# A clustered-attention and two-MLP kernel: the first pair's argmax by heads, wide similarity passes, joined output adds, a new order table

## The chip, the cores and the metric

The kernel runs on one core of a Trainium2 chip. The metric is the device time of one execution in microseconds. Three timed runs of the kernel before have a median of 694.74 us (693.54 to 695.31). The profiled execution took 693.93 us; its span, from the first to the last recorded instruction, is 692.1 us.

## The reference, cut to what matters

```python
# 2 batches, 8 heads, 768 tokens, head size 64, 16 cluster centroids per head
q_assign = argmax(einsum('bhsd,hcd->bhsc', normalised q, normalised c))     # nearest centroid of each query
k_assign = argmax(einsum('bhsd,hcd->bhsc', normalised k, normalised c))
mask     = q_assign[..., :, None] == k_assign[..., None, :]
attn     = softmax(where(mask, q @ k.T / 8, -1e9))
x        = attn @ v                                   # (1536 tokens, 512)
h        = max(x @ w1, x @ w2, x @ w3)                # 512 -> 768
x        = h @ w_out                                  # 768 -> 512
out      = relu(x @ w_in) ** 2 @ w_out2               # 512 -> 2048 -> 512
```

## The kernel before, in words

Products are made in float32r. An operand is split into a rounded part and the rest ("high" and "low"), and a product takes three passes (high·high, high·low, low·high) that are summed in PSUM.

**Attention part** (about the first 254 us). The 16 heads are 8 pairs (numbered 0 to 7, `p`); each head has 6 query tiles of 128 rows, so there are 96 tiles (`s`), handled in groups of three (`g`, 32 of them). For a pair: load q and k, split them (`p_rq`, `p_rk`, `p_lq`, `p_lk`), copy the pieces by DMA into the stacked operands of the score products (`p_stack`), multiply with the centroids (`p_sim`, two token halves), scale into SBUF (`p_simc`, ScalarE), transpose (`p_argt`), find the argmax in five VectorE steps (`p_arg0` to `p_arg4`) which leave a one-hot tile, transpose that (`p_mkt`), and put it as extra mask rows into the score operands (`p_mq`, `p_mk` directly for the first head; `p_m4` and the DMAs of `p_md` for the others). For a tile: scores on TensorE (`a_scores`, L729 and L731), row maximum on VectorE (`a_max`, L738), exponential with row sums on ScalarE (`a_exp`, L745), normalisation mostly on GpSimd (`a_norm`, L763). For a group: six times three transposes (`a_tr`, L768), the high part (`a_hi`, ScalarE, L774), the low part (`a_lo`, VectorE, L779), two products with v (`a_av`, L788 and L789).

In PSUM there are two double banks (psd) for score tiles, three banks (pss) for transposes, similarities, argmax and masks, and one bank for the product with v.

The order of all these steps, on all engines, is one written list, `ATT_ORDER`; each engine runs its own steps in that order. `warm(n)` puts n matmuls that compute nothing between steps at the start, `WARM` says how many.

**MLP part** (to the end). The order comes from a planner, `arrange`, which uses costs and due times, shifted by a second list (`MOE_LATER`). TensorE is the engine that is planned for. The last stage, `outs`, adds for each of 8 pieces of the inner dimension (`g`, NG = 8) and each of 12 token tiles (`tk`) a product (`out_mm`, L1321) to an accumulator in SBUF (`acc`), on VectorE (L1349) or by seeding the bank with the accumulator on ScalarE and copying it back (L1346). After the last piece each token tile is stored (L1352).

Of the kernel before, what the change touches and what calls it, by code (L numbers as in the profile page):

```python
# [1439 lines left out]
```

## Time and profile before

| | |
|---|---|
| median of three runs | 694.74 us |
| profiled execution | 693.93 us, span 692.1 us |
| TensorE (PE) busy | 676.9 us, 98% |
| VectorE (DVE) busy | 561.2 us, 81% |
| ScalarE (ACT) busy | 501.1 us, 72% |
| GpSimd (POOL) busy | 210.0 us, 30% |
| last product with v ends (attention ends on TensorE) | 253.9 us |
| last matmul ends | 687.2 us |

Shares are averages over stages: the attention stage loads four engines, the MLP stage TensorE above all. A busy TensorE is not one at its peak: a matmul's record lasts longer than the distance to the next one, so short stalls don't show as idle time. The distance between starts tells more.

### The profile page before, as it was taken

To read this page: it belongs to the slowest core of one execution; us is meant where nothing else is said; L and a number is where in the kernel's file an instruction comes from. 1 tells how busy PE (TensorE), PEld (TensorE's weight loads), DVE (VectorE), ACT (ScalarE), POOL (GpSimd) and SP (SyncE) were. 2 spreads that over 40 slices of the span, in tenths; PEclk is the share of its full clock that TensorE was granted. 3 is DMA by queue.
4 is the path that set the end of the run, shared out by engine and by line. 5 is a ranking of instruction groups with operands and counts; after the bars stand their busy time and mean duration, and the time that the engine had idled before them with its cause. 6 is when DMAs were issued, how large, how long until landed. Compare 5 with 4: busy or idle time off the path is not lost.

```text
span 692.1 us, 10148 instructions
## 1 busy us (share of the span) xinstructions
PE 676.9 (98%) x3531; PEld 577.3 (83%) x3531; DVE 561.2 (81%) x906; ACT 501.1 (72%) x977; POOL 210.0 (30%) x242
## 2 busy tenths in 40 slices
PE   7899999999999999999999999999999999999997
PEld 6689889899999878888888888888888888888885
DVE  6898999999999979998979659889679585968433
ACT  6899989899999865575545547798877786776610
POOL 6477987988769770100000000000000010000010
PEclk9999999999999999999999999999999999999999
DMA  7884553726432002211311231112211203120012
GB/s 207 198 234 119 120 161 91 189 58 147 111 89 91 1 1 93 91 62 61 103 66 61 76 121 62 61 62 82 101 62 61 98 27 115 48 79 1 1 73 111
DMA packets 22004, 62.21 MB, mean 90 GB/s; under 512 B 3616, under 2 KB 5280, under 8 KB 21504
## 3 DMA queue, kind: packets, MB, share of 16 engines
q1 hardware_dynamic: 21232, 59.98, 29.3%
q10 hardware_dynamic: 720, 1.57, 0.7%
q8 instruction: 28, 0.46, 0.3%
q14 instruction: 24, 0.20, 0.1%
HBM read 38.83 MB, written 3.15 MB: 61 GB/s over the span
## 4 chain that ended last, share of the span: by engine, by line
PE 62%; DVE 2%; issue 1%; ACT 1%; POOL 0%; ACTq 0%; POOLq 0%
PE pss L1066 23%; PE psn L1066 18%; PE pss L1321 10%; PE psn L1321 8%; PE pss L1142 1%; DVE acc_acc L1349 1%; DVE at L779 0%; DVE wtv L399 0%; PE pss L768 0%; ACT e L745 0%; PE pss L788 0%; PE pss L789 0%; POOL xT L822 0%; PE psn L1142 0%; PE psn L425 0%
## 5 line engine op out<-in xcount | busy, mean ns | idle before, releaser
L779 DVE TENSOR_TENSOR at<-pss,at 128x384 fp32r<-128x384 f32 x192 | 100.0, 548 | 13.1 <-ACT at L774 12.4
L763 POOL TENSOR_SCALAR e<-e,nm 128x768 f32<-128x768 f32 x93 | 85.6, 934 | 47.2 <-DVE nm L753 32.6
L738 DVE TENSOR_REDUCE nm<-psd 128x1 f32<-128x768 f32 x96 | 90.6, 948 | 5.4 <-PE psd L731 3.7
L774 ACT CAST at<-pss 128x384 fp32r<-128x384 f32 x192 | 86.5, 483 | 9.3 <-PE pss L768 7.4
L745 ACT ACTIVATE e<-psd,nm 128x768 f32<-128x768 f32 x96 | 87.3, 910 | 4.1 <-DVE nm L738 3.5
L768 PE MATMUL pss<-ident,e 128*128 128x128 f32 x576 | 86.5, 275 | 3.4 <-DVE at L779 1.7
L768 PEld LDWEIGHTS pss<-ident,e 128*128 128x128 f32 x576 | 68.6, 140 | 15.2 <-DVE at L779 5.0
L788 PE MATMUL pss<-at,vs 128*128 128x384 f32 x192 | 71.2, 371 | 0.5 <-ACT avt L801 0.5
L1321 PE MATMUL pss<-w_wh,g_g 128*128 128x512 f32 x216 | 71.4, 389 | 0.0
L789 PE MATMUL pss<-at,vs 128*128 128x384 f32 x192 | 65.8, 343 | 0.4 <-DVE at L779 0.3
L1057 POOL TENSOR_TENSOR t_tt<-a_a,t_tt 128x256 f32<-128x256 f32 x3 | 2.5, 848 | 191.5 <-DVE t_tt L1054 191.5
L1321 PE MATMUL psn<-w_wh,g_g 128*128 128x512 f32 (+1 forms) x172 | 56.5, 384 | 0.0
L1321 PEld LDWEIGHTS pss<-w_wh,g_g 128*128 128x128 f32 x216 | 40.5, 188 | 8.4
L1066 PE MATMUL pss<-xT,w_wh 128*128 128x512 f32 x140 | 43.1, 389 | 0.0
L1321 PE MATMUL pss<-w_wl,g_g 128*128 128x512 f32 x108 | 42.0, 389 | 0.0
L1042 ACT CAST w_wh<-a_a 128x1024 fp32r<-128x1024 f32 (+1 forms) x28 | 28.6, 1020 | 14.9 <-DVE a_a L1036 14.9
L789 PEld LDWEIGHTS pss<-at,vs 128*128 128x128 f32 x192 | 36.4, 189 | 3.0 <-DVE at L779 2.5
L1025 ACT ACTIVATE a_a<-raw_raw 128x512 f32<-128x512 f32 (+1 forms) x56 | 36.4, 653 | 3.3 <-DMA raw_raw<-w 1.3
L1321 PEld LDWEIGHTS psn<-w_wh,g_g 128*128 128x128 f32 x172 | 32.1, 188 | 6.4
L788 PEld LDWEIGHTS pss<-at,vs 128*128 128x128 f32 x192 | 36.2, 189 | 1.4 <-issue 0.5
L1027 ACT ACTIVATE r_r<-raw_raw 128x512 uint32<-128x512 uint32 (+1 forms) x56 | 36.5, 651 | 0.7 <-PE pss L1066 0.7
L1030 DVE SCALAR_TENSOR_TENSOR a_a<-raw_raw,a_a 128x512 uint32<-128x512 uint32 (+1 forms) x56 | 35.6, 668 | 0.5
(249 smaller groups left out, 1743.0 us busy)
## 6 DMA issues: line engine op xcount, KB each, us to landing
raw_raw<-w SPq DMA_DIRECT2D x16, 512.0 KB, 4.0
raw_raw<-win SPq DMA_DIRECT2D x16, 512.0 KB, 4.0
raw_raw<-wo SPq DMA_DIRECT2D x16, 512.0 KB, 3.6
raw_raw<-wo SPq DMA_DIRECT2D x8, 384.0 KB, 3.3
out<-acc_acc SPq DMA_DIRECT2D x11, 256.0 KB, 2.0
tv<-vv SPq DMA_DIRECT2D x7, 384.0 KB, 3.3
stodd<-rl SPq DMA_DIRECT2D x12, 192.0 KB, 5.5
stodd<-rl SPq DMA_DIRECT2D x4, 576.0 KB, 7.9
```

Of the source, the lines that this page charges most:

```text
L738: dve.tensor_reduce(nms[g][:, 0, i : i + 1], pss[s][:, :, :HS], axis=AX.XY, op=ALU.max, negate=True)
L745: act.activation(two(e), pss.pop(s)[:, :, :HS], AF.Exp, bias=nm[:, 0, i : i + 1], accum_out=nm[:, 1, i : i + 1])
L763: (pool if w == "P" else dve).tensor_scalar(e, e, r, 1.0, op0=ALU.mult, op1=ALU.mult)
L768: pe.transpose(pt[:, i * P : (i + 1) * P], et[3 * g + i][:, kt * P : (kt + 1) * P], ident)
L774: act.copy(a[:, 0, :], pts[g, kt][:, :HS])
L779: eng.tensor_tensor(a[:, 1, :], pts.pop((g, kt))[:, :HS], f(a[:, 0, :]), op=ALU.subtract)
L788: pe.matmul(avs[g][:, :HS], l, a[:, 0, :], start=kt == 0, stop=False)
L789: pe.matmul(avs[g][:, :HS], l, a[:, 1, :], start=False, stop=kt == NQ - 1)
L1025: op(("ab", u), due - 9, {A_: act_t(n) + 0.03}, lambda e, raw=raw, c=c: e.activation(T[a][:, c], f(T[raw][:, :n, 1]), AF.Abs), [("ld", u)] ...
L1027: op(("rd", u), due - 7.5, {A_: act_t(n) + 0.03}, lambda e, raw=raw, c=c: e.mul(u32(T[r][:, c]), T[raw][:, :n, 0], float(2.0**-29)), [("ld ...
L1066: pe.matmul(T[bank], T[w[wi]][:, wb * P : wb * P + P], x(xi), start=first and n == 0, stop=last and n == 3 * len(ks) - 1, skip_group_check ...
L1321: pe.matmul(T[bank][:, : n.stop - n.start], T["g", 2 * g + j, c][:, a_, i * P : i * P + P], T[wt, u][:, 512 * j + n.start : 512 * j + n.stop],
```

## The change

- **Argmax of pair 0 by heads.** Before, the five argmax steps ran once for each half of the tokens (both heads). Now they run once for the first head of the pair (`o` = 0) and once for the second; each of them needs all tokens. The mask transposes of the first head's keys (two halves) and queries come right after the first five steps and go into tiles of their own; the query mask uses a double bank of the score tiles. The tile for the second head is made later. Mask rows are written in pieces by VectorE and ScalarE.
- **Tile 1 in two single banks** (`SPLIT`): its scores go into two banks of the transposes, with two maxima and two exponentials and small steps that join them. In group 0 each tile is normalised by itself, all three on GpSimd (before: two on ScalarE).
- **Similarities in four passes** for pairs 1 to 7 (`WIDE = 1`): the centroids' high and low parts stand side by side, and one pass with 128 stationary columns makes two results in different partitions, which a new VectorE step (`p_simd`) adds. Pair 0 keeps six passes.
- **Low part of q** (`p_lq`) for pairs 1 to 7 in one step instead of two; one of pair 0's low parts of k moves to GpSimd. The two copies at the end of a group (`a_fin_copy`) become steps of their own.
- **Joined adds**: for four token tiles (8, 10, 0, 2) the products of the last two pieces stay in one bank, and one add brings both to the accumulator. Token tile 2 is stored in two halves (before: token tile 3's last product was halved).
- **Warm-up**: the matmuls use a tile of ones instead of the identity; other counts, some of them placed by `PE_FILL` inside the order list.
- **A new `ATT_ORDER`.** In the MLP part all engines keep their order but for the last output tiles.

VectorE, from the first argmax step to the first row maximum of the score tiles, before (tiles pss_69: the transposed similarities; ste: the score operand of the first head; nm: row maxima):

```order
L653 TENSOR_REDUCE mx_247<-pss_69 128x12
L662 TENSOR_TENSOR pss_69<-pss_69,tieb 128x192
L658 TENSOR_TENSOR pss_69<-pss_69,mx_247 128x192
L667 TENSOR_REDUCE m_295<-pss_69 128x12
L662 TENSOR_TENSOR pss_69<-pss_69,tieb 128x192
L673 TENSOR_TENSOR oh_299<-pss_69,m_295 128x192
L667 TENSOR_REDUCE m_295<-pss_69 128x12
L673 TENSOR_TENSOR oh_299<-pss_69,m_295 128x192
L697 CAST ste_228<-pss_71 16x384 x2
L553 SCALAR_TENSOR_TENSOR xT<-tq_209,xT 128x384
L738 TENSOR_REDUCE nm_360<-psd_76 128x1
```

And the same stretch of VectorE now, from the first head's one-hot (oh) on:

```order
L702 TENSOR_TENSOR oh_300<-pss_69,m_294 128x12x16
L687 TENSOR_REDUCE mx_282<-pss_69 128x12
L691 TENSOR_TENSOR pss_69<-pss_69,mx_282 128x12x16
L695 TENSOR_TENSOR pss_69<-pss_69,tieb 128x12x16
L737 CAST ste_231<-pss_70 16x384
L699 TENSOR_REDUCE m_294<-pss_69 128x12
L732 TENSOR_SCALAR ste_231<-psd_80 16x128
L702 TENSOR_TENSOR oh_300<-pss_69,m_294 128x12x16
L785 TENSOR_REDUCE nm_361<-psd_76 128x1
L788 TENSOR_REDUCE nm_361<-pss_70 128x1
L788 TENSOR_REDUCE part<-pss_71 128x1
```

The first one-hot now stands ahead of the second head's steps, two pieces of mask rows (L737, L732) stand among those, and the maximum of tile 0 follows at once; the low part of pair 1's q (L553 before) has moved behind it.

TensorE, tiles 2 to 5 of the first head and the similarities of pair 1 (cb: centroids), before:

```order
L613 MATMUL pss_69<-xT,cb 64x384 x6
L729 MATMUL psd_76<-ste_228 128x384 x2
L731 MATMUL psd_76<-ste_228 128x384 x2
L729 MATMUL psd_80<-ste_228 128x384 x2
L731 MATMUL psd_80<-ste_228 128x384 x2
L729 MATMUL psd_76<-ste_228 128x384 x2
L731 MATMUL psd_76<-ste_228 128x384 x2
L613 MATMUL pss_70<-xT,cb 64x384 x6
```

And now, tiles 4 and 5 (tiles 2 and 3 stand ahead of both similarities):

```order
L633 MATMUL pss_69<-xT,cb 128x384 x2
L633 MATMUL pss_69<-xT,cb 64x384 x2
L774 MATMUL psd_80<-ste_231 128x384 x2
L776 MATMUL psd_80<-ste_231 128x384 x2
L633 MATMUL pss_70<-xT,cb 128x384 x2
L633 MATMUL pss_70<-xT,cb 64x384 x2
```

Six passes became four, two of them with 128 output partitions, and they moved behind tile 3.

VectorE, the last adds to the accumulators, before:

```order
L1349 TENSOR_TENSOR acc_acc_5127<-pss_71,acc_acc_5127 128x512
L1349 TENSOR_TENSOR acc_acc_5176<-pss_69,acc_acc_5176 128x512
L1349 TENSOR_TENSOR acc_acc_5176<-pss_70,acc_acc_5176 128x512
L1349 TENSOR_TENSOR acc_acc_5214<-psn_3410,acc_acc_5214 128x512
L1349 TENSOR_TENSOR acc_acc_5214<-psn_3240,acc_acc_5214 128x512
L1349 TENSOR_TENSOR acc_acc_5252<-psn_3411,acc_acc_5252 128x512
L1349 TENSOR_TENSOR acc_acc_5252<-psn_3241,acc_acc_5252 128x512
```

And now:

```order
L1433 TENSOR_TENSOR acc_acc_5187<-psn_3423,acc_acc_5187 128x512
L1433 TENSOR_TENSOR acc_acc_5225<-pss_71,acc_acc_5225 128x512
L1433 TENSOR_TENSOR acc_acc_5263<-pss_70,acc_acc_5263 128x512
L1433 TENSOR_TENSOR acc_acc_5263<-pss_72,acc_acc_5263 128x256
L1433 TENSOR_TENSOR acc_acc_5263<-psn_3424,acc_acc_5263 128x256
```

The pairs of adds to one accumulator are gone, and two half-width adds stand last.

The diff, cut to its core:

```diff
-WARM = 12, 34, 0, 28, 10, 14, 0
+WARM = 20, 22, 0, 26, 0, 0, 0
+SPLIT = 1,
-    "lk@0": "D", "nrm": "PPP", "nrm@0": "AAP", ...
+    "lk@0": "PD", "lq@0": "D", "nrm": "PPP", "nrm@0": "PPP", ...
+WIDE = 1
+PE_FILL = {38: 16, 56: 9, 62: 12}
 ATT_ORDER = [
-    4, 7, 5, 6, 11, 12, 8, 9, 50, 13, 20, 14, 0, 16, 22, 3, ...
+    7, 4, 6, 12, 5, 8, 9, 11, 52, 15, 13, 20, 14, 0, 16, 22, 3, ...
...
         def p_lq(p, hf):
-            c = slice(hf * HS, hf * HS + HS)
+            c = slice(0, S) if p else half(hf)
...
-            for w, hs, ls in ((slice(32, 96), 0, 3), (slice(0, 64), 1, 2)):
-                ops += [(cb[:, 0, hp, w], rl[:, hs, c]), (cb[:, 0, hp, w], rl[:, ls, c]), (cb[:, 1, hp, w], rl[:, hs, c])]
-            for i, (l, r) in enumerate(ops):
-                pe.matmul(pt[0:64, :HS], l, r, start=i == 0, stop=i == 5)
+            for w, hs, ls in ((32, 0, 3), (0, 1, 2)):
+                ops += [(w, 64, ls), (w, 128, hs)] if p >= WIDE else [(w, 64, hs), (w, 64, ls), (w + 64, 64, hs)]
+            ops.sort(key=lambda o: -o[1])
+            for i, (w, n, x) in enumerate(ops):
+                pe.matmul(pt[0:n, :HS], cb[:, hp, w : w + n], rl[:, x, c], start=i == 0, stop=i == len(ops) - 1, skip_group_check=True)
...
+        def p_simd(p, hf):
+            r = slice(64 * hf, 64 * hf + 64)
+            t = simt[p][r]
+            dve.scalar_tensor_tensor(t, psims[p, hf][r, :HS], scl[r, p % HP : p % HP + 1], t, op0=ALU.mult, op1=ALU.add)
...
+        def p_mkt(p, i=None):
...
+            if i == 2:
+                pt = pmk["q"] = rings["S"][1][:, 0, :].bitcast(BF16)
+            else:
+                pt = pmk["k", i] = ps_m(f"pmk{p}_{i}", BF16)
+            for t in range(NQ):
+                if i > 1 or t // (NQ // 2) == i:
+                    c = slice(0, 64) if i == 3 else slice(0, 16) if i == 2 else slice(32, 48)
+                    pe.transpose(pt[0 : c.stop - c.start, t * P : (t + 1) * P], o[:, t, c], identb)
...
+            if s in SPLIT:
+                pt = [ps_t(f"ps{s}_{hf}")[:, :HS] for hf in range(2)]
...
+    JOINT = 8, 10, 0, 2
...
+            joint = g >= NG - 2 and tk in JOINT
+            for n in ([slice(0, 256), slice(256, 512)] if joint and tk == JOINT[-1] else [slice(0, 512)]):
+                bank = ("ps", "o", NG - 1 if joint else g, tk, n.start)
...
+                if joint and g < NG - 1:
+                    continue
```

## Rows read from the trace of the kernel before

**Rows 1.** The page, span, busy time of TensorE (PE) and weight loads (PEld)

```profile
span 692.1 us, 10148 instructions
...
PE 676.9 (98%) x3531; PEld 577.3 (83%) x3531; DVE 561.2 (81%) x906; ACT 501.1 (72%) x977; POOL 210.0 (30%) x242
```

**Rows 2.** Windows: stretch, its length, busy us (x instructions) of each engine, clock, DMA

```profile
15.00:50.00 35.00, 31.70 (x197) 26.47 (x198) 31.03 (x54) 30.46 (x66) 21.39 (x25) 1.00 0.82 211
60.00:200.00 140.00, 138.65 (x917) 128.31 (x916) 129.67 (x231) 132.47 (x311) 116.54 (x125) 1.00 0.51 126
...
300.00:650.00 350.00, 350.00 (x1546) 289.78 (x1545) 273.49 (x394) 238.77 (x401) 4.87 (x5) 1.00 0.20 70
...
687.00:688.00 1.00, 0.16 (x1) 0.00 (x0) 0.97 (x3) 0.00 (x0) 0.00 (x0) 1.00 0.45 174
```

**Rows 3.** Timeline of TensorE at 150 us: start us, us, instruction, operands, count

```profile
150.13 1.21 PE L613 MATMUL pss<-rl,cb 128*64 128x384 f32 x6
151.18 0.52 PE L729 MATMUL psd<-stodd 128*128 128x384 f32 x2
151.53 0.52 PE L731 MATMUL psd<-stodd 128*128 128x384 f32 x2
```

**Rows 4.** Groups by line, 60 to 200 us: count | busy us, mean ns | idle before

```profile
L779 DVE TENSOR_TENSOR at<-pss,at 128x384 fp32r<-128x384 f32 x118 | 61.4, 549 | 6.8 <-ACT at L774 6.3
L763 POOL TENSOR_SCALAR e<-e,nm 128x768 f32<-128x768 f32 x60 | 54.6, 925 | 22.1 <-DVE nm L753 18.1 <-PE pss L682 2.0 <-PE pss L768 0.9
...
L789 PEld LDWEIGHTS pss<-at,vs 128*128 128x128 f32 x118 | 22.4, 189 | 1.0 <-DVE at L779 0.8
...
L613 PEld LDWEIGHTS pss<-xT,cb 128*64 128x64 f32 x36 | 4.8, 135 | 1.1
...
L553 DVE SCALAR_TENSOR_TENSOR rl<-tq,rl 128x384 fp32r<-128x384 f32 x4 | 3.8, 941 | 0.0
...
L553 DVE SCALAR_TENSOR_TENSOR xT<-tq,xT 128x384 fp32r<-128x384 f32 x4 | 2.9, 713 | 0.0
```

**Rows 5.** Line L553 over the whole span: count, shortest/median/longest ns

```profile
L553 DVE SCALAR_TENSOR_TENSOR rl<-tq,rl x8: 528/564/1227, 5.0 to 148.4; 128x384 fp32r<-128x384 f32 x8
```

**Rows 6.** Timeline of TensorE at the start

```profile
3.73 3.23 PE L325 MATMUL pss<-identb 128*128 128x128 bf16 x34
6.77 2.29 PE L613 MATMUL pss<-rl,cb 128*64 128x384 f32 x12
...
16.11 0.52 PE L731 MATMUL psd<-ste 80*128 80x384 f32 x2
...
24.47 1.07 PE L768 MATMUL pss<-ident,e 128*128 128x128 f32 x6
```

**Rows 7.** Timeline of VectorE at the start

```profile
9.42 0.36 DVE L653 TENSOR_REDUCE mx<-pss 128x12 f32<-128x192 f32 x1 [1.33 <-PE pss L644]
...
13.37 0.36 DVE L673 TENSOR_TENSOR oh<-pss,m 128x192 bf16<-128x192 f32 x1
```

**Rows 8.** Timeline of ScalarE at the start

```profile
8.19 0.58 ACT L619 ACTIVATE simt<-pss,scl 64x384 f32<-64x384 f32 x1 [1.13 <-DVE scl L503]
...
15.02 1.22 ACT L694 ACTIVATE ste<-pss,m4b,m4s 16x384 fp32r<-16x384 bf16 x2 [2.61 <-PE pss L690]
...
22.97 1.75 ACT L761 ACTIVATE e<-e,nm 128x768 f32<-128x768 f32 x2
```

**Rows 9.** Groups by line, 0 to 50 us, GpSimd

```profile
L559 POOL TENSOR_TENSOR rl<-tk,rl 128x384 fp32r<-128x384 f32 x2 | 2.0, 1009 | 0.1
```

**Rows 10.** The chain that ended last, its end: start us, us, what

```profile
681.69 1.40 PE pss L1321 x6
...
686.56 1.34 DVE acc_acc L1349 x2
...
687.92 0.69 DVE acc_acc L1349
```

**Rows 11.** Line L1349, 660 us on: shortest/median/longest ns, the shortest is the half width

```profile
L1349 DVE TENSOR_TENSOR acc_acc<-psn,acc_acc x8: 415/692/693, 665.4 to 687.9; 128x512 f32<-128x512 f32 x6, 128x256 f32<-128x256 f32 x2
```

More of the change, by code (lines that the diff above doesn't have):

```diff
@@ L290, in single_banks @@
     def single_banks(i):
-        pd[i].close()
-        one = ctx.enter_context(tc.tile_pool(name=f"pn{i}", bufs=1, space=PSUM, side=SIDES[i]))
+        o = (i + len(SPLIT)) % 2
+        pd[o].close()
+        one = ctx.enter_context(tc.tile_pool(name=f"pn{i}", bufs=1, space=PSUM, side=SIDES[o]))
         psu[i][:2] = [one.tile([P, 512], F32, name=f"psn{2 * i + j}") for j in range(2)]
@@ L314, in clustered_attention_moe @@
     identb = ac.tile([P, P], BF16, name="identb")
+    ones = ac.tile([P, P], BF16, name="ones")
+    dve.memset(ones, 1.0)
     tieb = ac.tile([P, NC], BF16, name="tieb")
@@ L324, in warm @@
         for _ in range(n):
-            pe.matmul(ps1[3][:, :P], identb, identb, start=True, stop=True)
+            pe.matmul(ps1[3][:, :P], ones, ones, start=True, stop=True)
     warm(WARM[0])
@@ L498, in clustered_attention_moe @@
         cs = ap1.tile([P, 4], F32, name="cs")
-        scl = ap1.tile([64, HP], F32, name="scl")
+        scl = ap1.tile([P, HP], F32, name="scl")
         def c_scale(eng, i):
-            for r in (0, 32):
+            for r in range(0, P, 32):
                 eng.tensor_copy(scl[r : r + 32, i : i + 1], cs[32 * i : 32 * i + 32, 3:4])
@@ new lines, in p_mkt, with p_mq @@
+            for t in range(NQ):
+                if i > 1 or t // (NQ // 2) == i:
+                    c = slice(0, 64) if i == 3 else slice(0, 16) if i == 2 else slice(32, 48)
+                    pe.transpose(pt[0 : c.stop - c.start, t * P : (t + 1) * P], o[:, t, c], identb)
+            if i == 3:
+                pmk[p] = pt
+            warm(WARM[4])
+        QS = [slice(0, P), slice(P, S)]
+        def p_mq(p, i):
+            to, fr = st[0][64:80, 1, QS[i]], pmk["q"][0:16, QS[i]]
+            if i == 0:
+                dve.tensor_scalar(to, fr, BIG, -BIG, op0=ALU.mult, op1=ALU.add)
+            else:
+                act.activation(to, fr, AF.Identity, bias=m4b[0:16], scale=m4s[0:16])
@@ L720, in clustered_attention_moe @@
         et, nms, pss, ats, avs, xraw, pts = {}, {}, {}, {}, {}, {}, {}
+        part = ap1.tile([P, 2], F32, name="part")
         def a_scores(s):
@@ L724, in a_scores @@
             t = st[h]
-            pt = ps_s(f"ps{s}")
+            if s in SPLIT:
+                pt = [ps_t(f"ps{s}_{hf}")[:, :HS] for hf in range(2)]
+            else:
+                pt = ps_s(f"ps{s}")
+                pt = [pt[:, hf, :HS] for hf in range(2)] + [pt[:, :, :HS]]
             k2 = slice(0, 80) if h % 2 == 0 else slice(0, 128)
@@ L737, in a_max @@
                 nms[g] = ap.tile([P, 4, 3], F32, tag="nm", bufs=4, name=f"nm{g}")
-            dve.tensor_reduce(nms[g][:, 0, i : i + 1], pss[s][:, :, :HS], axis=AX.XY, op=ALU.max, negate=True)
+            m = nms[g][:, 0, i : i + 1]
+            if s not in SPLIT:
+                dve.tensor_reduce(m, pss[s][2], axis=AX.XY, op=ALU.max, negate=True)
+                return
+            for hf, to in enumerate((m, part[:, 0:1])):
+                dve.tensor_reduce(to, pss[s][hf], axis=AX.X, op=ALU.max, negate=True)
+            dve.tensor_tensor(m, m, part[:, 0:1], op=ALU.min)
         def a_exp(s):
@@ L744, in a_exp, with a_sum, a_guard, a_rec @@
             nm = nms[g]
-            act.activation(two(e), pss.pop(s)[:, :, :HS], AF.Exp, bias=nm[:, 0, i : i + 1], accum_out=nm[:, 1, i : i + 1])
-        def a_guard(g):
-            nm = nms[g]
-            act.activation(nm[:, 2, :], nm[:, 1, :], AF.Identity, bias=guard)
-        def a_rec(g):
-            nm = nms[g]
-            dve.reciprocal(nm[:, 3, :], nm[:, 2, :])
+            pt, m, sm = pss.pop(s), nm[:, 0, i : i + 1], nm[:, 1, i : i + 1]
+            if s not in SPLIT:
+                act.activation(two(e), pt[2], AF.Exp, bias=m, accum_out=sm)
+                return
+            for hf, to in enumerate((sm, part[:, 1:2])):
+                act.activation(e[:, half(hf)], pt[hf], AF.Exp, bias=m, accum_out=to)
+        def a_sum(s):
+            g, i = divmod(s, 3)
+            sm = nms[g][:, 1, i : i + 1]
+            dve.tensor_tensor(sm, sm, part[:, 1:2], op=ALU.add)
+        def a_guard(g, i=None):
+            nm, c = nms[g], slice(0, 3) if i is None else slice(i, i + 1)
+            act.activation(nm[:, 2, c], nm[:, 1, c], AF.Identity, bias=guard)
+        def a_rec(g, i=None):
+            nm, c = nms[g], slice(0, 3) if i is None else slice(i, i + 1)
+            dve.reciprocal(nm[:, 3, c], nm[:, 2, c])
         def a_norm(s):
@@ L870, in clustered_attention_moe @@
                      opens=[("sm", p, 0)] if hf == 0 else (), uses=[("T", "sim", p, hf), ("sm", p, 0)])
+                if p >= WIDE:
+                    pop_("simd", p_simd, (p, hf), [("simc", p, hf)], uses=[("T", "sim", p, hf), ("sm", p, 0)])
+            sims = [("simd" if p >= WIDE else "simc", p, h) for h in range(2)]
             for hf in hv:
-                first = hf != (1,)
-                sim = [("simc", p, h) for h in (hf or (0, 1))]
-                pop_("argt", p_argt, (p, *hf), sim, opens=[("T", "arg", p)] * first, uses=[("sm", p, 0), ("T", "arg", p)])
@@ new lines, in clustered_attention_moe @@
+            if p == 0:
+                for i in range(4):
+                    pop_("mkt", p_mkt, (p, i), [("arg4", p, i // 3)] + [("mkt", p, i - 1)] * (i > 0), opens=[("T", "mk" if i == 3 else f"mk{i}", p)] * (i != 2), uses=[("oh", p)])
+                for hf in range(2):
+                    pop_("mk", p_mk, (p, hf), [("mkt", p, hf), ("stack", p, 0)], uses=[("T", f"mk{hf}", p)])
+                for i in range(2):
+                    pop_("mq", p_mq, (p, i), [("mkt", p, 2), ("stack", p, 0)])
+            else:
+                pop_("mkt", p_mkt, (p,), [("arg4", p)], opens=[("T", "mk", p)], uses=[("oh", p)])
@@ L953, in clustered_attention_moe @@
             fn(*args)
+            warm(PE_FILL.get(x, 0))
     NCH = NTOK // 512
@@ L1328, in outs @@
             c = tk // 4
-            last = g == NG - 1 and i == len(tks) - 1
-            for n in ([slice(0, 256), slice(256, 512)] if last else [slice(0, 512)]):
-                bank = ("ps", "o", g, tk, n.start)
+            joint = g >= NG - 2 and tk in JOINT
+            for n in ([slice(0, 256), slice(256, 512)] if joint and tk == JOINT[-1] else [slice(0, 512)]):
+                bank = ("ps", "o", NG - 1 if joint else g, tk, n.start)
                 opn = ("om", g, tk, n.start)
@@ L1338, in outs @@
                     op(("sd", g, tk), at - 1.5, {A_: 0.525}, lambda e, bank=bank, tk=tk: seed(T[bank], acc(tk)), [("oa", g - 1, tk, 0)], [("ps", bank)], [bank, to])
+                adds = seeded or joint and g < NG - 1
                 op(opn, at + 0.01 * n.start, {"pe": 6 * (w_ + 32) / 2400},
-                   lambda _, bank=bank, g=g, tk=tk, n=n, seeded=seeded: out_mm(bank, g, tk, n, not seeded),
-                   [("wl", u)] + [("lo", "g", 2 * g + j, c) for j in range(2)] + ([("sd", g, tk)] if seeded else []), () if seeded else [("ps", bank)],
+                   lambda _, bank=bank, g=g, tk=tk, n=n, adds=adds: out_mm(bank, g, tk, n, not adds),
+                   [("wl", u)] + [("lo", "g", 2 * g + j, c) for j in range(2)] + ([("sd", g, tk)] if seeded else [("om", g + 1, tk, n.start)] if adds else []),
+                   () if adds else [("ps", bank)],
                    [("wh", u), ("wl", u), bank] + [("g", 2 * g + j, c) for j in range(2)])
+                if joint and g < NG - 1:
+                    continue
+                done_by = [("om", g - 1, tk, n.start), ("oa", g - 2, tk, 0)] if joint else [opn, ("oa", g - 1, tk, 0)]
                 if g == 0 or seeded:
```

166 lines of the change are left out of this document (83 added, 83 removed), and 251 rows, old and new, of tables (ATT_ORDER, ENG, MOE_LATER).

## The prediction

> **What bounds the kernel now.** I read the page first: TensorE is busy for 98% of the span [rows 1]. The table of windows then splits that into stages [rows 2], and the reader is to see three different kernels in it. From 300 to 650 us TensorE is busy for all of 350 us and the other engines have slack: only matmuls count there. In the same order table the MLP part stays as it was but for the last output tiles, and it holds the same products, so I cost that stage at nothing. From 60 to 200 us, where five pairs go by (28.0 us each), four engines are full: TensorE 138.65, ScalarE 132.47, VectorE 129.67 and GpSimd 116.54 of 140 us, per pair 27.7, 26.5, 25.9 and 23.3. From 15 to 50 us TensorE passes 197 matmuls, 5.6 per us, against 917 in 140 us, 6.5 per us, later: there it starves, and its busy time of 31.70 of 35 us doesn't show how much. At that rate 197 matmuls would take 30 us, so about 5 us are lost there.
>
> The timelines at the start show what the first scores wait for [rows 6 to 8], the chain of waits its last link, VectorE's adds behind TensorE [rows 10]. Whether a steady TensorE has room between matmuls I took from distances of starts: at 150 us six similarity passes start within 1.05 us and two score passes within 0.35 us [rows 3], 0.175 us each, no gap. So in the steady attention stage TensorE ends last, with ScalarE and VectorE 1.5 and 2 us per pair behind it.
>
> The sum is made against the profiled execution, 693.93 us (span 692.1 and 1.8 us around it). The median of the runs is 694.74, 0.8 more; the forecast is put on that.
>
> **The start.** Before, the similarities begin at 6.77 us, when 34 warm-up matmuls end (3.73 + 3.23, with the pipeline's overlap) [rows 6]. Twelve fewer warm-up matmuls of 0.09 us take 1.1 us off that, but the operands hold it: the low part of k's first half goes to GpSimd, where it takes 1.0 us [rows 9], while VectorE has one subtraction less in its queue. I count 0.7 us. The scaling begins at 8.19 us because it waits for VectorE's scale [rows 8]; that comes earlier by the subtraction and two small steps moved up, later by two more small copies: 0.5 us gained. The argmax ran from 9.42 to 13.73 us in ten steps of 0.36 us and the waits between them [rows 7]. Now the first head's five steps are done after about 2.0 us (five times 0.36, plus 0.04 each of distance), but they start only when both halves are transposed, about when VectorE's second half began before (0.6 us later). So the first head's one-hot comes about 1.7 us sooner than the last one did, and with the 0.5 us in front 2.2 us. Behind it are twelve small transposes instead of six for the keys and queries, the mask pieces on two engines, and three of the second head's steps ahead of VectorE's first piece: there is nothing to gain. ScalarE had two pieces in 1.22 us [rows 8]; now one smaller and one longer, about 1.4. The masked second half of the first scores was issued at 16.11 us [rows 6]; I put it at 13.9, 2.2 us sooner. Bounds: 0, if the mask chain takes back the gain, and 3.0, if the transposes hide behind the copies.
>
> The first group's transposes start at 24.47 us, held by two normalisations on ScalarE, 1.75 us from 22.97 [rows 6, 8]. Three on GpSimd take 0.925 us each [rows 4], but each may go when its own tile is ready, so only the last counts: about 0.9 instead of 1.75 us. Against that, VectorE gets two maxima of half width and five tiny steps for tile 1. I call this even, and the start 2.2 us.
>
> **The steady stage.** Each of seven pairs loses four passes, 4 x 0.175 = 0.70 us of TensorE, in all 4.9. VectorE gets two adds of 64x384 out of PSUM per pair; the nearest row is the low part L779, 118 in 61.4 us, 0.52 each [rows 4], so 1.04 per pair. The joined low part of q gives some back: its rows last 0.83 us on average (941 and 713 over four each), but 0.53 at the shortest and 1.23 at the longest [rows 4, 5], the same work, so about 0.3 of each is waiting. One such wait less leaves +0.74 per pair. Bounds for VectorE: +1.04 with nothing back, +0.4 with a start and a whole long wait saved.
>
> After the change a pair costs TensorE 27.0, VectorE 26.7 and ScalarE 26.5 us. Three engines within 0.5 us can't all be kept full: each needs a result of the other two. A bank of a similarity is also held longer, by one VectorE step and its place in that queue, out of three that the transposes use; what waits behind it on TensorE are the next transposes. So of 4.9 us I take 2.0, where the slack that VectorE and ScalarE lose is about the same share as TensorE's relief; bounds 4.9 and a loss of 3 (the seven adds' 7.3 us less the idle time that takes half of it).
>
> About the 128-column pass the trace shows that a load of 64 columns lasts 135 ns and one of 128 columns 189 ns [rows 4], and that passes with 128-column loads still start 0.175 us apart, as those with 64 do [rows 3]. The Trainium skill (TensorE: Matmul & The Clock Gate, section "LDWEIGHTS (loading the stationary operand)") says that a load's time goes with its columns, not with the rows. By the rule alone four wide loads a pair cost 4 x 0.054 = 0.2 us, in all 1.5 us; by the distances they cost nothing, and these decide.
>
> The skill's page "SBUF — State Buffer" (section "SBUF: two separate sides") says that a VectorE step with two SBUF inputs and a GpSimd step share a port pair that one of them holds for its whole instruction. The spread of L553's rows from 0.53 to 1.23 us [rows 5] agrees; by the rule the joined step holds GpSimd twice as long at one go, which GpSimd, idle 23.5 of 140 us, bears.
>
> **The junction.** The chain from the last product with v over GpSimd to the first product of the MLP part keeps its steps, so what the attention part gains is passed on whole.
>
> **The tail.** The last matmul ends at 687.16 [rows 2], the last add at 687.92 + 0.69 = 688.61 [rows 10]: VectorE is 1.45 us behind, because each last token tile needs two adds of 0.69 us, about the 1.40 us of its six matmuls [rows 10]. With joined adds VectorE has one per 2.7 us of matmuls and only the half-width add of 0.415 us [rows 11] is left, with 0.1 us to its start: 0.95 gained. Twelve more half-width matmuls (24 of about 0.12 us, half of a whole one, for 12 of them and 6 whole ones of 0.23) cost 0.1. I take 0.9; bounds 0, if the last store lands no sooner, and 1.4.
>
> **Sum.** 2.2 + 2.0 + 0.9 = 5.1 us: span 687.0, profiled execution 688.8, median 689.6.
>
> **The rivals.**
> First, TensorE's relief comes through whole: 3.0 + 4.9 + 1.4 = 9.3, median 685.4. For it speaks that TensorE is the fullest engine; against it, how close the others are.
>
> Second, the start is swallowed: VectorE is busy 31.03 of 35 us from 15 to 50 [rows 2] and gets four of the new adds there (2.1 us), just the gain, and ScalarE, at 26.5 per pair, holds the rest. What is left is the tail: median 693.8. For it speaks that VectorE, not TensorE, paces that stretch; against it that the scores come sooner and 4 us of VectorE's time there is idle.
>
> Third, slower: VectorE becomes the bound and keeps the idle time it has now. That is (140 - 129.67)/5 = 2.07 us per pair, mostly waits for ScalarE's high part, 6.3 us in all [rows 4]. A pair then takes 25.9 + 1.04 + 2.07 = 29.0, 1.0 more, over seven pairs 7.3, less start and tail, 3.1: median 694.74 + 4.2 = 698.9. It decides from an idle time of 1.5 us per pair, where 7 x (26.97 + 1.47 - 28.0) is 3.1. Against it: the waits are those of an order, and the order is new.
>
> That the change doesn't do what it says is excluded by the rows of the order: four passes, joined adds and the earlier mask pieces stand there.
>
> **How the numbers follow.** The forecast (part of the relief) gets 0.56, with its own range from 687 to 692.5; the whole relief 0.18; the swallowed start 0.15; VectorE as the bound 0.11. The range of 8 in 10 leaves out about half of the first rival and all of the third: 685.3 to 694.8. A measurement of this kernel can tell 0.3%, 2.1 us, from no change: faster is below 692.7, which holds for the forecast and the first rival, 0.74; the second is the same, 0.15; the third slower, 0.11.
>
> **What would show it.** In the changed profile: the masked half of the first scores near 13.9 us, the first group's transposes near 22 us; the product with v ending near 249.7 (253.9 less 4.2), so the MLP part starting that much earlier, with no idle TensorE from there to the end; VectorE's share in the steady stage near 95%; similarity passes in fours 0.7 us long; the last add 0.5 us behind the last matmul. The forecast is wrong if the steady pair takes longer than 28.0 us or if TensorE's start shows new gaps where the fills stand.

## The result, and the profile after

The changed kernel takes 687.57 us (median of 4 runs, 687.46 to 688.59) against 694.50 us in the runs of the kernel before beside it: a ratio of 0.9903, 95% interval 0.9892 to 0.9915, or 6.9 us less. The forecast was 689.6 us, within a range of 685.3 to 694.8. The profiled execution took 687.66 us, with a span of 685.5 us against 692.1.

Two marks split both spans into start, attention and the rest: the first transposes of the first group, and the 24 matmuls of the MLP part that begin once the attention part's last result is there. Of before, the timeline of TensorE shows the second mark so (start us, us, instruction, operands, count, and in brackets the idle time before it; the first mark is in [rows 6]):

```profile
259.82 0.73 PE L1142 MATMUL psn<-xT,whl 128*128 128x512 f32 x2 [0.20 <-POOL xT L822]
260.39 5.62 PE L1142 MATMUL pss<-xT,whl 128*128 128x512 f32 x24
```

The same view of after, at the start and at the end of the attention part:

```profile
3.71 2.55 PE L338 MATMUL pss<-ones 128*128 128x128 bf16 x22
6.02 2.91 PE L633 MATMUL pss<-rl,cb 128*64 128x384 f32 x12
...
14.38 0.61 PE L776 MATMUL psd<-ste 80*128 80x384 f32 x2
...
22.03 1.65 PE L829 MATMUL pss<-ident,e 128*128 128x128 f32 x9
...
247.55 0.44 PE L850 MATMUL pss<-at,vs 128*128 128x384 f32 x1
247.83 4.92 PE L438 MATMUL psn<-xT,whl 128*128 128x512 f32 x21
252.59 0.39 PE L1218 MATMUL psn<-xT,whl 128*128 128x512 f32 x1
253.93 0.74 PE L1218 MATMUL psn<-xT,whl 128*128 128x512 f32 x2 [0.95 <-POOL xT L881]
254.51 5.65 PE L1218 MATMUL pss<-xT,whl 128*128 128x512 f32 x24
```

| part of the span | before | after | difference | forecast |
|---|---|---|---|---|
| start, to the first transposes | 24.47 | 22.03 | -2.44 | -2.2 |
| attention, to the 24 matmuls | 235.92 | 232.48 | -3.44 | -2.0 |
| MLP part and tail | 431.71 | 430.99 | -0.72 | -0.9 |

The windows of after (stretch, its length, busy us and instructions of TensorE, its weight loads, VectorE, ScalarE, GpSimd, then clock and DMA) answer to [rows 2]:

```profile
15.00:50.00 35.00, 32.36 (x213) 27.06 (x214) 34.29 (x63) 30.41 (x71) 23.34 (x27) 1.00 0.85 211
60.00:200.00 140.00, 138.05 (x902) 126.45 (x901) 133.51 (x239) 133.24 (x314) 117.03 (x128) 1.00 0.50 125
...
300.00:650.00 350.00, 350.00 (x1546) 289.85 (x1545) 271.71 (x393) 239.45 (x402) 4.85 (x5) 1.00 0.20 68
```

VectorE rose from 129.67 to 133.51 of 140 us while TensorE hardly moved; the MLP part is as full as before. The groups of VectorE from 60 to 200 us (count | busy us, mean ns | idle before them) answer to [rows 4]:

```profile
L840 DVE TENSOR_TENSOR at<-pss,at 128x384 fp32r<-128x384 f32 x119 | 61.8, 547 | 3.6 <-ACT at L835 3.3
...
L646 DVE SCALAR_TENSOR_TENSOR simt<-pss,scl,simt 64x384 f32<-64x384 f32 x10 | 6.2, 615 | 0.4 <-ACT simt L641 0.2
...
L571 DVE SCALAR_TENSOR_TENSOR xT<-tq,xT 128x768 fp32r<-128x768 f32 x2 | 1.9, 939 | 0.0
L571 DVE SCALAR_TENSOR_TENSOR rl<-tq,rl 128x768 fp32r<-128x768 f32 x2 | 1.9, 938 | 0.0
```

The new add takes 0.62 us (forecast 0.52, which was the busy time of the low part L779 divided by its count; that row's mean of one was 0.549). The joined low part of q takes 0.94 us, where its halves took 0.94 and 0.71 each. VectorE's wait for ScalarE's high part fell from 6.3 to 3.3 us. A similarity is now four passes in 0.69 us (133.38 to 134.07), against 1.05 for six [rows 3]:

```profile
133.38 0.86 PE L633 MATMUL pss<-rl,cb 128*128 128x384 f32 x4
134.07 0.51 PE L774 MATMUL psd<-ste 128*128 128x384 f32 x2
```

At the start, VectorE's first argmax step comes later than before and its first head is done at 11.98 us; ScalarE's first mask piece follows at 12.57 instead of 15.02 [rows 7, 8]:

```profile
10.03 0.36 DVE L687 TENSOR_REDUCE mx<-pss 128x12 f32<-128x192 f32 x1 [2.03 <-PE pss L666]
...
11.62 0.36 DVE L702 TENSOR_TENSOR oh<-pss,m 128x192 bf16<-128x192 f32 x1
```

```profile
12.57 0.47 ACT L737 CAST ste<-pss 16x384 fp32r<-16x384 bf16 x1 [0.29 <-PE pss L722]
12.94 0.87 ACT L734 ACTIVATE ste<-psd,m4b,m4s 16x640 fp32r<-16x640 bf16 x1
```

At the end, the last matmul and, on VectorE, the last adds (the answer to [rows 10]):

```profile
681.10 0.28 PE L1397 MATMUL psn<-w_wh,g_g 128*128 128x256 f32 x1
```

```profile
680.61 1.02 DVE L1433 TENSOR_TENSOR acc_acc<-pss,acc_acc 128x512 f32<-128x512 f32 x2 [1.29 <-ACT acc_acc L1430]
681.54 0.41 DVE L1433 TENSOR_TENSOR acc_acc<-psn,acc_acc 128x256 f32<-128x256 f32 x1
```

The last add ends at 681.95, 0.57 us behind the last matmul's 681.38; before it was 1.45.

### The profile page after: what moved, and what is told of

Same layout as the page of the kernel before. It is cut to its first block, busy times and chain, and to the rows that moved or that the text cites. A ratio compares the mean times of both kernels' runs of the same rounds, so it can differ in the third digit from the quotient of the medians.

```text
span 685.5 us, 10164 instructions
## 1 busy us (share of the span) xinstructions
PE 673.5 (98%) x3522; PEld 575.3 (84%) x3522; DVE 559.2 (82%) x916; ACT 499.6 (73%) x979; POOL 212.4 (31%) x251
## 4 chain that ended last, share of the span: by engine, by line
PE 82%; DVE 10%; ACT 3%; POOL 1%; issue 1%; DMA 1%; DVEq 0%; ACTq 0%; POOLq 0%
PE pss L1142 24%; PE psn L1142 19%; PE pss L1397 11%; PE psn L1397 8%; PE pss L829 6%; DVE nm L785 3%; DVE at L840 3%; PE pss L850 3%; PE pss L849 3%; PE psd L774 3%; PE psd L776 3%; ACT at L835 1%; PE pss L633 1%; ACT e L798 1%; PE pss L1218 1%
## 5 line engine op out<-in xcount | busy, mean ns | idle before, releaser
L824 POOL TENSOR_SCALAR e<-e,nm 128x768 f32<-128x768 f32 x95 | 87.1, 930 | 36.3 <-DVE nm L814 22.6
L1397 PE MATMUL pss<-w_wh,g_g 128*128 128x512 f32 (+1 forms) x232 | 75.6, 385 | 0.0
L1397 PE MATMUL psn<-w_wh,g_g 128*128 128x512 f32 (+1 forms) x160 | 53.1, 384 | 0.0
L1397 PEld LDWEIGHTS pss<-w_wh,g_g 128*128 128x128 f32 x232 | 43.4, 188 | 8.8
L1397 PE MATMUL pss<-w_wl,g_g 128*128 128x512 f32 (+1 forms) x116 | 44.7, 386 | 0.0
L1120 DVE TENSOR_TENSOR w_wl<-a_a,w_wh 128x1024 fp32r<-128x1024 f32 (+1 forms) x28 | 34.0, 1214 | 1.6 <-ACT w_wh L1118 0.9
```

The costliest lines, as they stand in the source:

```text
L824: (pool if w == "P" else dve).tensor_scalar(e, e, r, 1.0, op0=ALU.mult, op1=ALU.mult)
L1397: pe.matmul(T[bank][:, : n.stop - n.start], T["g", 2 * g + j, c][:, a_, i * P : i * P + P], T[wt, u][:, 512 * j + n.start : 512 * j + n.stop],
```

## The experiments

Every run starts from the changed kernel, with one or more things undone, added or doubled. "Stretch" is the attention part between the two marks, of one profiled execution: it leaves out what the start does, which varies by 1.4 us from run to run (in the four executions with the same start and the same steps, the first transposes stood between 21.3 and 22.7 us). The changed kernel's stretch is 232.5 us, its median 687.57. Beside the runs the kernel before had medians from 694.2 to 694.7 us, so medians of two runs within half a microsecond don't tell them apart.

| run | first transposes | stretch | median of the runs |
|---|---|---|---|
| before | 24.47 | 235.92 | 694.50 |
| changed | 22.03 | 232.48 | 687.57 |
| late start | 22.48 | 232.55 | 688.99 |
| no fill | 21.82 | 232.50 | 687.99 |
| old tail | 21.31 | 232.49 | 687.67 |
| six passes, add kept | 22.56 | 234.27 | 690.06 |
| four passes, no add | 21.49 | 231.39 | 686.42 |
| four passes, add twice | 21.99 | 240.02 | 695.33 |
| six passes, no add | 22.62 | 234.11 | 688.83 |
| q's low part in halves | 21.36 | 233.45 | 688.39 |
| old steps, new order | 22.96 | 233.70 | 689.00 |
| old steps, old order | 21.91 | 238.19 | 693.31 |
| new steps, old order | 21.29 | 243.26 | 698.87 |
| the same, adds later | 22.69 | 245.03 | 699.97 |

### The start

```diff
-WARM = 20, 22, 0, 26, 0, 0, 0
+WARM = 20, 46, 0, 26, 0, 0, 0
```

> The changed kernel with 24 more warm-up matmuls before the first similarities, which then start about 2.5 us later, near 8.5 us. Theory (a start that is later by so much is later at the end by as much): 2.5 us slower, 690.1. Rival (the loaded engines of the first pair swallow it): 0 to 1 us slower, 687.6 to 688.6.

The similarities started at 7.08 us, 1.06 later and not 2.5: the warm-up matmuls speed up on the way, 12 from 4 to 5 us and 22 from 6 to 7 (the windows' rows):

```profile
4.00:5.00 1.00, 1.00 (x12) 1.00 (x11) 0.81 (x5) 0.84 (x4) 0.92 (x2) 1.00 0.44 155
...
6.00:7.00 1.00, 1.00 (x22) 1.00 (x19) 0.97 (x4) 0.99 (x2) 1.00 (x2) 1.00 0.57 147
```

In the profiled execution the first transposes moved by 0.45 us and the span by 0.5 (686.0), with the same stretch of 232.55 us. So behind the same order a start that is later by half a microsecond is later at the end by as much. Without the 24 more, the similarities start anywhere from 5.53 to 6.87 us in the profiled executions, so this run made the start hardly later than chance does. Stronger is that the four executions with the changed kernel's steady stage (changed, late start, no fill, old tail) have first transposes from 21.31 to 22.48 us and stretches from 232.48 to 232.55. The median, 1.4 us up, doesn't contradict it, but the other runs' starts weren't profiled.

```diff
-PE_FILL = {38: 16, 56: 9, 62: 12}
+PE_FILL = {}
```

> The changed kernel without the 37 fill matmuls in three places of the start. Theory (they stand in waits and nothing depends on them): within 0.7 us of 687.6, first group's transposes at 21.3 to 22.0 us. Rival (without them TensorE's granted clock falls in the start): a granted clock below 1.00 between 10 and 25 us, transposes at 23 us or later, median 689 or more.

687.99 us, ratio to before 0.9913 (0.9900 to 0.9925): no difference that can be told. From 10 to 25 us TensorE is busy for 12.34 instead of 14.05 us, and its granted clock is 1.00 in both. No effect of the fills shows here.

### The tail

```diff
-    JOINT = 8, 10, 0, 2
...
-            joint = g >= NG - 2 and tk in JOINT
+            last = g == NG - 1 and i == len(tks) - 1
```

(with the last tiles' banks, adds and offsets of the kernel before)

> The changed kernel with the last output tiles and the offsets of the MLP part as in the kernel before: every tile of the last two groups has an add of its own. Theory (the tail's gain is the adds' lag less what the last store takes longer): 0.8 us slower than the changed kernel, 688.4. Rival (the last store hides it): within 0.3 us of 687.6.

The median, 687.67, is 0.1 us above the changed kernel's, within the scatter of the starts. The trace tells more: from the 24 matmuls (253.80) to the end of the span (685.6) it takes 431.8 us. The kernel before takes 431.7, and all eleven other profiled variants, like the changed kernel, 431.0 to 431.1. So the tail is worth 0.7 us, by the traces; the medians can't show it (in its profiled execution the first transposes came 0.72 us earlier than in the changed kernel's, which hides just as much).

### The steps of the steady stage

Two passes more, with the adds kept:

```diff
             ops.sort(key=lambda o: -o[1])
+            if p >= WIDE:
+                for w, x in ((32, 3), (0, 1)):
+                    pe.matmul(pt[0:64, :HS], cb[:, hp, w : w + 64], rl[:, x, c], start=True, stop=True, skip_group_check=True)
```

> The changed kernel with VectorE's adds kept and two 64-column passes put ahead of each similarity of pairs 1 to 7, which the next pass overwrites: six passes again, +0.70 us of TensorE per pair, 4.9 in all; the result is the same. Theory (TensorE paces): 3.5 to 5 us slower than the changed kernel, about 691.5. Rival (VectorE paces, TensorE has slack): at most 1.5 us slower, 687.6 to 689.

690.06 us, 2.5 more; stretch +1.8. That lies between the theory's and the rival's numbers: of 4.9 us of TensorE, 1.8 arrive.

The add left out:

```diff
         def p_simd(p, hf):
...
-            dve.scalar_tensor_tensor(t, psims[p, hf][r, :HS], scl[r, p % HP : p % HP + 1], t, op0=ALU.mult, op1=ALU.add)
+            pass
```

> The changed kernel with four passes for pairs 1 to 7, but VectorE's add is left out, so the low part of the centroids is missing from the similarities of these pairs. VectorE has 8.6 us less, TensorE the same work. Theory (TensorE paces): 686 to 687.6, at most 1.5 us faster than the changed kernel. Rival (VectorE paces): 5 to 8.6 us faster, 679 to 682.6.

686.42 us, 1.2 less (its runs scatter from 685.5 to 688.9); stretch -1.1, as in the theory. The adds' 8.6 us of VectorE cost the stretch 1.1.

The add done twice (the line above stands there two times):

> The changed kernel with each of VectorE's adds of pairs 1 to 7 done twice, so the low part counts double in the similarities: 14 more steps of 0.62 us, 8.6 us of VectorE. Theory (TensorE paces, VectorE has 6.5 us of idle time in 140): 1 to 3 us slower than the changed kernel, 688.6 to 690.6. Rival (VectorE paces): 6 to 8.6 us slower, 693.6 to 696.

695.33 us, 7.8 more; stretch +7.5: here the rival's number holds. The windows of this run show why both runs can be true:

```profile
60.00:200.00 140.00, 134.84 (x868) 121.44 (x868) 135.17 (x242) 130.08 (x301) 114.66 (x124) 1.00 0.51 126
```

VectorE is at 135.17 of 140 us and TensorE falls to 134.84. Of the first 8.6 us of adds each microsecond cost 0.13 us, of the next 8.6 us 0.87. The likely reading is that the changed kernel stands right at the point where VectorE becomes the bound. That is argued, not shown: the second add also makes the chain from a similarity to its argmax longer and holds the bank longer, and in this run TensorE waits 1.9 of 140 us for that second add.

Six passes and no add:

```diff
-                ops += [(w, 64, ls), (w, 128, hs)] if p >= WIDE else [(w, 64, hs), (w, 64, ls), (w + 64, 64, hs)]
+                ops += [(w, 64, hs), (w, 64, ls), (w + 64, 64, hs)]
...
-            r = slice(64 - 64 * hf, 128 - 64 * hf) if p >= WIDE else slice(0, 64)
+            r = slice(0, 64)
```

(and the add left out as above)

> The changed kernel and its order, but pairs 1 to 7 take their similarities in six 64-column passes and VectorE's add is left out (the result is the same). Per pair TensorE has 0.70 us more and VectorE two adds of 0.62 us less, over seven pairs +4.9 and -8.6 us. Theory (TensorE's passes pace the steady stage, the adds lie in VectorE's slack): slower than the changed kernel by about 3.5 us, 691. Rival (VectorE, at 95% of the steady stage, paces it): faster by 4 us or more, 683 or less. If both hold the stage about equally: within 1.5 us of 687.6.

688.83 us, 1.3 more; stretch +1.6: the third case. Neither of the two engines holds the stage alone, and the trade of passes for adds is worth 1.3 to 1.6 us.

```diff
         def p_lq(p, hf):
             rl = prep[p]
-            c = slice(0, S) if p else half(hf)
-            dve.scalar_tensor_tensor(rl[:, 3, c], ins[p][0][:, c], 0.125, f(rl[:, 0, c]), op0=ALU.mult, op1=ALU.subtract)
+            for c in [half(0), half(1)] if p else [half(hf)]:
+                dve.scalar_tensor_tensor(rl[:, 3, c], ins[p][0][:, c], 0.125, f(rl[:, 0, c]), op0=ALU.mult, op1=ALU.subtract)
```

> The changed kernel with q's low part of pairs 1 to 7 again in two instructions of half the width, both where the joined one stands. By the rows VectorE has 2 x 0.83 instead of 0.95 us per pair, 4.9 us more over seven pairs. Theory (VectorE is at its limit, as the doubled adds cost 0.9 us per us): 3 to 4.5 us slower than the changed kernel, 690.6 to 692. Rival (only the adds that stand in the similarities' chain cost, VectorE's load as such does not): at most 1 us slower, 687.6 to 688.6.

688.39 us, 0.8 more; stretch +1.0. The expected 4.9 us of VectorE weren't there, since the halves no longer take 0.83 us where they now stand (mean ns of one, 60 to 200 us):

```profile
L571 DVE SCALAR_TENSOR_TENSOR rl<-tq,rl 128x384 fp32r<-128x384 f32 x4 | 2.6, 697 | 0.3 <-DMA tk<-kT 0.3
L571 DVE SCALAR_TENSOR_TENSOR xT<-tq,xT 128x384 fp32r<-128x384 f32 x4 | 2.0, 546 | 0.0
```

That is 1.24 us per pair, 0.3 more than joined. The rival's number was met, but the run doesn't separate the two theories; it shows that more than half of the gain of 0.7 us per pair on this step (0.4) comes from its place and not from the joining. The run with old steps, further down, adds something: there, without the adds, the halves cost nothing (stretch 233.70, with the joined step 234.11). So what a step of VectorE costs depends on how full VectorE is, which speaks for the first theory but leaves the second add's longer chain untested.

### The order

The steps stay, the order goes back, behind the start:

```diff
 ATT_ORDER = [
...
-    ..., 287, 69, 725, 278, 720, 722, 298, ...
+    ..., 287, 69, 725, 726, 278, 70, 282, 727, 71, 288, ...
```

> The changed kernel with all its steps, and with its order as far as the 125th step (some 30 us, the whole start); from there the steps stand in the order of the kernel before, with each add right behind its scaling, the joined low part of q where its first half stood, and the two copies of a product with v side by side. Theory (the new order is what turns the shorter queue into time): slower than the changed kernel by 1.5 to 4 us, 689 to 691.6. Rival (what counts is that TensorE and VectorE have less to do, whatever the order): within 0.7 us of 687.6.

698.87 us: 11.3 us slower than the changed kernel, and slower than before (ratio 1.0068, 1.0054 to 1.0082), far beyond both numbers. The stretch takes 10.8 us more. TensorE is busy for only 132.65 of 140 us, and VectorE has 11.8 us of idle time, although it has the same work:

```profile
60.00:200.00 140.00, 132.65 (x859) 120.25 (x858) 128.19 (x228) 127.83 (x297) 114.06 (x124) 1.00 0.48 120
```

Its groups there (VectorE, then TensorE's transposes; after the second bar the idle time before them):

```profile
L843 DVE TENSOR_TENSOR at<-pss,at 128x384 fp32r<-128x384 f32 x113 | 58.5, 547 | 4.8 <-ACT at L838 4.3
...
L649 DVE SCALAR_TENSOR_TENSOR simt<-pss,scl,simt 64x384 f32<-64x384 f32 x10 | 6.2, 616 | 5.9 <-ACT simt L644 5.8
...
L574 DVE SCALAR_TENSOR_TENSOR rl<-tq,rl 128x768 fp32r<-128x768 f32 x2 | 3.0, 1508 | 0.1
```

```profile
L832 PE MATMUL pss<-ident,e 128*128 128x128 f32 x342 | 51.7, 276 | 5.4 <-DVE at L843 2.5 <-DVE simt L649 1.9 <-POOL xr L872 0.7
```

The adds wait 5.8 us for the scaling ahead of them, and TensorE waits for VectorE. Some of that is for banks: the transposes L832 read no similarity, so when the profile has them wait for an add (1.9 us), it can only be for the bank that the add still reads. Are the adds' own waits the cause? The adds moved behind later steps of VectorE, eleven of the fourteen; here one of them (153):

```diff
-    ..., 175, 152, 153, 928, 947, 960, ...
+    ..., 175, 152, 928, 947, 153, 960, ...
```

> The run with the new steps in the old order took 243.3 us from the first group's transposes to the MLP part, 10.8 more than the changed kernel; VectorE's adds waited 5.8 us of 140 for the scaling on ScalarE right ahead of them. Here only that is changed: each add stands behind the next step of VectorE that follows its scaling, two to eight places later. Theory (the wait of the adds at the head of VectorE's queue is most of the loss: 5.8 x 7/5 = 8.1 us): 235 to 239 us for the stretch, median 691 to 695. Rival (the loss comes from the banks that the adds hold, or from the joined step): 242 us or more, median 697.5 or more.

699.97 us, stretch 245.0: no gain, and that theory fell. (In this execution the mean granted clock was 0.76 from 132 to 136 us and 0.82 from there to 140, between the levels of 1.2 and 2.4 GHz, after TensorE had been busy for 3.12 of 4 us. The missing share of the clock over these 8 us is 1.7 us, an estimate of the most that it cost; without it the stretch would still be 243.3.) The add's own wait went, but VectorE's wait for the high part rose from 4.3 to 7.4 us and that of TensorE's transposes for the adds from 1.9 to 3.6:

```profile
L843 DVE TENSOR_TENSOR at<-pss,at 128x384 fp32r<-128x384 f32 x111 | 57.7, 549 | 7.8 <-ACT at L838 7.4
...
L649 DVE SCALAR_TENSOR_TENSOR simt<-pss,scl,simt 64x384 f32<-64x384 f32 x10 | 6.1, 614 | 0.9 <-ACT simt L644 0.7
```

```profile
L832 PE MATMUL pss<-ident,e 128*128 128x128 f32 x333 | 50.0, 276 | 5.1 <-DVE simt L649 3.6 <-DVE at L843 1.3 <-DVE oh L705 0.2
```

That fits the rival's first half (banks are held until the add is done), though how much of the 10.8 us it makes isn't shown. Its other half, the joined step, is small: two of four took 1.51 instead of 0.94 us in these 140 us, 1.1 us of VectorE in all. Which of the old order's places cost the 10.8 us stays open.

Old steps in the old order, behind the new start:

```diff
-                ops += [(w, 64, ls), (w, 128, hs)] if p >= WIDE else [(w, 64, hs), (w, 64, ls), (w + 64, 64, hs)]
+                ops += [(w, 64, hs), (w, 64, ls), (w + 64, 64, hs)]
```

(with the add left out, q's low part in halves and the old order, all as above)

> The changed kernel's start (its order as far as the 125th step) and its tail, but behind that the steps and the order of the kernel before: six-pass similarities, no adds of VectorE, q's low part in two instructions. From the first group's transposes to the MLP part the kernel before took 235.9 us, the changed one 232.5. Theory (start and tail pass to the end whole, the rest is the steady stage): 235.9 us for that stretch again, and 2.4 (start) + 0.8 (tail) less than before, about 691.2. Rival (the steady stage swallows the earlier start): 693.5 or more.

693.31 us (ratio 0.9990, 0.9979 to 1.0000), and the stretch is 238.2, not 235.9: of the 2.6 us that the start gained, 2.3 were given back. In the table of windows the loss stands in places: from 106 to 134 us TensorE is busy for 25.87 of 28 us, where it was 27.88 before (before first):

```profile
106.00:134.00 28.00, 27.88 (x185) 25.55 (x183) 26.61 (x47) 26.40 (x63) 22.31 (x24) 1.00 0.55 137
```

```profile
106.00:134.00 28.00, 25.87 (x172) 23.66 (x171) 25.99 (x46) 24.69 (x58) 20.01 (x22) 1.00 0.52 134
```

The rival (693.5 or more) was missed by 0.2 us, the theory (691.2) by 2.1. It looks as if an order made for one start did not suit the other; a bad seam at the 125th step, where the two orders were joined, would look the same and wasn't tested.

Old steps in the new order (the three edits without the order's):

> The changed kernel with its new order throughout, but the old steps for pairs 1 to 7: six-pass similarities, no adds of VectorE, q's low part in two instructions. Theory (the runs with one of these undone add up: +1.6 and +1.0 us in the stretch from the first group's transposes to the MLP part): 235.1 us for the stretch, median about 690.2; so new steps and new order are worth little alone. Rival 1 (the new order is worth the 10.8 us of the run with the old order, whatever the steps): 225 us, median about 680. Rival 2 (an order made for other steps costs): 237 us or more, median 692 or more.

689.00 us; stretch 233.7. Neither rival's 225 nor 237 us; the single runs' sum, 235.1, is 1.4 too high. Without the adds the halves of q's low part cost nothing, so the effects don't add up.

So the two things that the change does to the steady stage, by their stretches:

| | old steps | new steps |
|---|---|---|
| old order | 238.2 (with the old start 235.9) | 243.3 |
| new order | 233.7 | 232.5 |

The marks of the three cells that have no rows above are, in order: new order with old steps, old order with old steps, old order with new steps.

```profile
22.96 1.15 PE L829 MATMUL pss<-ident,e 128*128 128x128 f32 x9
...
256.66 5.61 PE L1218 MATMUL pss<-xT,whl 128*128 128x512 f32 x24
```

```profile
21.91 1.15 PE L832 MATMUL pss<-ident,e 128*128 128x128 f32 x9
...
260.10 5.61 PE L1221 MATMUL pss<-xT,whl 128*128 128x512 f32 x24
```

```profile
21.29 1.64 PE L832 MATMUL pss<-ident,e 128*128 128x128 f32 x9
...
264.55 5.62 PE L1221 MATMUL pss<-xT,whl 128*128 128x512 f32 x24
```

In the old order the new steps cost 5.1 us; in the new order they give 1.2. With old steps the new order gives 4.5 us against the same start, 2.2 against the kernel before. Each stretch is from one execution; the four of the changed steady stage agree within 0.07 us.

## Why the prediction was right, and where it was not

**The start** (2.2 us, measured 2.44): the path was right, the close agreement is partly luck. The forecast had all of the 2.2 us ahead of the masked half of the first scores and called the rest even. The masked half was put at 13.9 us; it stood at 14.38, a gain of 1.73, and in the ten other profiled executions with this start and its fills at 13.6 to 15.0 (13.6 to 14.2 where the twelve similarity passes take 2.3 instead of 2.9 us). From there to the first group's transposes it took 8.36 us before and 7.65 now (7.66 and 7.67 in the three other executions with the same start and steps): the part called even gave 0.7. The first transposes were put near 22 us and started at 22.03; with the same start they stood from 21.3 to 22.7, a gain of 1.8 to 3.2 us against the one execution of before. The similarities gained 0.75 us (forecast 0.7): in the changed kernel they follow the warm-up without a gap, and without the fills their first pass ran at 5.56 us and the others waited 0.49 us for q's low part, so warm-up and operands are about even there. From run to run the similarities started at 5.53 to 6.87 us. That the gain arrives whole is shown behind the new order; behind the old one, the run with old steps kept 0.3 of 2.6 us.

**The steady stage** (2.0 us, measured 3.44) is the step that failed in its size: "of 4.9 us I take 2.0, where the slack that VectorE and ScalarE lose is about the same share as TensorE's relief". It took the gain from the steps alone and counted the order only as an argument against the slower rival. The runs show 1.2 us for the steps in the new order and 2.2 for what else changed in this part, above all the order. This split goes by one path; by the other, the steps alone, in the old order, cost 5.1 us, which the forecast's "same share" had no place for. VectorE's load per pair rose by 1.23 - 0.71 = 0.52 us by the rows of its steps, less than the forecast +0.74 and within its bounds. Two errors went against each other: the add is 0.62 and not 0.52 us, and the joined low part saves 0.7 and not 0.3 us, since nearly all of its waiting went. (The windows' 133.51 - 129.67 is 0.77 per pair, but the later one holds a tile more, 61 row maxima instead of 60.) The lower bound, a loss of 3, was also added up too small: half of 7.3 is 3.65. The 128-column passes cost nothing extra: four start 0.17 us apart.

**The junction** passed the gain on whole: the product with v ended 5.9 us earlier (at 247.99 us, where the forecast said 249.7), the 24 matmuls started 5.9 us earlier. The product that waits for GpSimd there waits 0.95 instead of 0.20 us, ahead of the second mark.

**The tail** (0.9 us, measured 0.72): the lag fell by 0.88 (forecast 0.95), the twelve half-width matmuls cost 0.1 as forecast (from the 24 matmuls to the last matmul's end 426.77 before, 426.87 after), and the last store ended 0.06 us later behind its add.

**The rivals** are worth a look, since two of their prices were met by other kernels. "Start swallowed, only the tail left", 693.8: the run with old steps and old order took 693.31. But the price was met without the rival's reason: that run has no adds, and its loss stands from 106 to 134 us, not from 15 to 50. "VectorE becomes the bound and keeps its idle time", 698.9: the run with new steps in the old order took 698.87, with 11.8 us of VectorE idle in 140, or 2.4 us in a pair of some 28.9 us (28.0 scaled by the stretch). This comes near the rival's mechanism (2.07 us idle), though more of the idle time is waits for the scaling than for the high part (5.8 and 4.3 us), and that the totals agree to 0.03 us is chance. The prediction said that this case decides from 1.5 us idle per pair; in the changed kernel it is 6.5 of 140 us, 1.3 per pair of 27.5 us. What kept it away is the new order: the steps are the same. The first rival, the whole relief, is excluded for the new order: TensorE's 4.9 us are worth 1.8.

## What to carry to other kernels

When three engines are each busy for 95% or more of a stage, price a traded step twice: in the old order and in an order made for it. Here the same steps cost 5 us in the one and gave 1 us in the other, so no sum over durations alone could tell the sign. To compare variants whose start scatters, use marks in the trace: a stretch between two marks repeated within 0.07 us where the starts of the same steps scattered by 1.4 us.

## What the runs showed of the hardware that was not expected

The prediction named the spread of L553; what a bad place costs a joined step, and GpSimd beside it, the runs showed. In the run with the old order the joined low part took 1.62 us, where it takes 0.95 alone, and GpSimd's subtraction behind it 1.71 instead of 1.0:

```profile
129.32 1.62 DVE L574 SCALAR_TENSOR_TENSOR rl<-tq,rl 128x768 fp32r<-128x768 f32 x1
```

```profile
129.11 1.01 POOL L884 TENSOR_TENSOR xT<-xr,xT 128x384 fp32r<-128x384 f32 x1
130.08 1.71 POOL L580 TENSOR_TENSOR rl<-tk,rl 128x384 fp32r<-128x384 f32 x1
```

In the changed kernel the same step of the same pair stands where GpSimd waits for TensorE, and takes 0.95 us:

```profile
130.70 0.95 DVE L571 SCALAR_TENSOR_TENSOR rl<-tq,rl 128x768 fp32r<-128x768 f32 x1
```

```profile
131.93 1.80 POOL L824 TENSOR_SCALAR e<-e,nm 128x768 f32<-128x768 f32 x2 [3.13 <-PE pss L829]
```

These rows agree with the Trainium skill ("SBUF — State Buffer", section "SBUF: two separate sides"), by which the one that comes second waits for the whole instruction of the first: 129.11 + 1.01 = 130.12, and 0.95 us more is 131.07, near the 130.94 at which the step ended.

An add of 64 partitions with an operand in PSUM and one in SBUF and a scale per partition took 0.62 us, more than the 0.55 us of a plain subtraction of 128 partitions and the same 384 columns. Whether the partitions count at all isn't shown, as the operations differ.

The same 128-column matmuls went at 12 and then at 22 per microsecond in the start (rows above, late start), with a granted clock of 1.00 in both stretches; the similarities' 2.3 to 2.9 us from run to run may be the same effect. No run here shows its cause.
